# Sigmoid attention with a gated FFN on one core: where batch 0's first FFN chunks stand among its scores and value products

## The chip, the core and the metric

One core of one Trainium2 chip runs the whole program. The metric is the device time in microseconds from one execution; runs are given by their median. TensorE (PE) does the matrix products, ScalarE (ACT) the sigmoids, VectorE (DVE) most copies out of PSUM, GpSimd (POOL) issues the loads, SyncE (SP) the stores and DMA transposes. TensorE's weight loads are a row of their own (PEld) and overlap its matmuls.

## The reference

```python
def _attn_ref(q, k, v):                       # batch 8, heads 12, seq 448, head_dim 64
    scores = scale * np.matmul(q, k.transpose(0, 1, 3, 2)) - np.log(S)
    attn = 1.0 / (1.0 + np.exp(-scores))
    return np.matmul(attn, v)

def _moe_ref(x, w_gate, w_val, w_out):        # x: 3584 x 768, d_ff 1536
    gate = np.maximum(x @ w_gate, 0.0)
    val = x @ w_val
    return gate * val @ w_out
```

The attention output, with its heads joined, is x. Each score goes through a sigmoid by itself, so there is no sum over a row and no rescaling: a value product can begin as soon as the sigmoids of its first keys are done. Inputs and result are 32-bit floats; the kernel computes in 16-bit floats with 32-bit sums.

## The kernel before

**Attention.** A batch has 12 heads, taken as three groups g of four heads; a head's 448 positions are 7 chunks of 64. The scores are made with the keys on the partitions: four matmuls of 64x64 weights at a time, one in each quarter of the array (`qk`, L232). Queries and keys must first be turned (`pe_transposes`, L194): matmuls against an identity into PSUM, then copied to `qkT` by VectorE. ScalarE's sigmoid (L186) takes the scores from PSUM to a 16-bit tile `PT`. The value product (`pv`, L248) runs over the 7 key chunks in order, 28 matmuls in two banks; VectorE scales the two banks into `xT` (`put_xT`, L176), the FFN's input.

**FFN.** d_ff is 12 chunks f of 128. For a chunk, `gv` makes the gate product and the value product (six matmuls each over the 768 input features, one bank each), then the relu of the gate and the product of the two, which goes to `hT`. Batches 0 and 1 make their chunks this way. From batch 2 on other functions (`gv_pair`, `down_pair`) do it for two batches together; they are not touched here.

**Batch 0 in slots.** Nothing is there to overlap with at the start, so batch 0 is cut finer: its queries into a first part of 256 columns and a second of 192. There are six slots (`FirstSlot`, L269): slots 0, 1, 2 are groups 0, 1, 2 with the first query part, slots 3, 4, 5 the same groups with the second. A slot has four units of two key chunks (the last has one): a unit makes scores into one of two pairs of PSUM banks (`pairp`, two buffers), and one sigmoid takes them out. A slot's value product needs the sigmoids of all its four units. Chunk f of the FFN for the first query part needs the value products of slots 0, 1 and 2; chunk f for the second part needs those of slots 3, 4 and 5.

**What sets the order.** The program is scheduled by hand: each engine does its instructions in the order in which the code emits them, and waits at an instruction whose inputs or buffers aren't ready. The order around the change is the table `after`: its entry (i, u) is what is emitted behind unit u of slot i. `ffn_mix(n)` takes n chunks from the queue `gv_queue`. Matrix products other than the units' scores take PSUM banks from a ring of four (`bank`), each reused four takes later. For the first four chunks relu and product are both done by VectorE (`act_relu` False).

**Loads.** All loads of batch 0, of the gate and value weights (`load_gv`, in pieces by chunks: 0 and 1, 2 and 3, 4 and 5, 6 to 8, 9 to 11) and of batch 1 are issued by GpSimd ahead of this stretch in its own order. From the ninth on, a load is issued when the eighth before it has landed.

Of the kernel before, what the change touches and what calls it, by code (L numbers as in the profile page):

```python
# [17 lines left out]
def kernel(  # L18
# [10 lines left out]
    nc = tc.nc  # L29
# [5 lines left out]
    P = 128  # L35
    NCH = S // 64
    NDC = DM // P
# [3 lines left out]
    HALVES = ((0, QCUT), (QCUT, NCH))  # L41
# [34 lines left out]
    def bank(name, shape=(P, 512), dtype=FP32):  # L76
        pool, tag = free[0]
        free.rotate(-1)
        return pool.tile(list(shape), dtype, tag=tag, name=name)
# [60 lines left out]
    wg = wpool.tile([P, NDC, DF], FP16, name="wg")  # L140
    wv = wpool.tile([P, NDC, DF], FP16, name="wv")
# [26 lines left out]
    xT_tiles = {}  # L168
# [25 lines left out]
    def pe_transposes(b, g, ti, c0=0, c1=NCH):  # L194
        transposed(b, g, ti, c0, c1)()

    def transposed(b, g, ti, c0, c1):
        t16 = in_tiles[b][ti]
        qkT = qkT_of(b, g)
        trt = bank16("trt")  # L200
        for c in range(c0, c1):
            for h in range(2):
                nc.tensor.transpose(  # L203
                    trt[64 * h : 64 * h + 64, c * P : (c + 1) * P],
                    t16[:, 2 * g + h, c * D : (c + 1) * D],
                    ident[:],
                )

        def copy(a0=c0, a1=c1):
            nc.vector.tensor_copy(  # L210
                qkT[:, ti * NCH + a0 : ti * NCH + a1, :].rearrange("p c x -> p (c x)"),
                trt[:, a0 * P : a1 * P],
            )

        return copy
# [92 lines left out]


    def gv(b, q0, qn, f, act_relu):  # L310
        gv_out(b, q0, qn, f, act_relu, [gv_product(b, q0, qn, f, i) for i in range(2)])

    def gv_two(b, q0, qn, f):
        ps = [[gv_product(b, q0, qn, f + u, i) for u in range(2)] for i in range(2)]
        for u in range(2):
            gv_out(b, q0, qn, f + u, False, (ps[0][u], ps[1][u]))

    def gv_product(b, q0, qn, f, i):
        ps = bank(("g_ps", "v_ps")[i])
        for dc in range(NDC):  # L320
            nc.tensor.matmul(  # L321
                ps[:, 0:qn],
                (wg, wv)[i][:, dc, f * P : (f + 1) * P],
                xT_tiles[b][:, dc, q0 : q0 + qn],
                start=(dc == 0),
                stop=(dc == NDC - 1),
            )
        return ps

    def gv_out(b, q0, qn, f, act_relu, ps):  # L330
        gate_sb = gsbp.tile([P, S], FP32, tag="gsb", name="gate_sb")
        if act_relu:
            nc.scalar.activation(gate_sb[:, 0:qn], ps[0][:, 0:qn], AF.Relu)
        else:
            nc.vector.tensor_scalar(
                out=gate_sb[:, 0:qn], in0=ps[0][:, 0:qn], scalar1=0.0, scalar2=None, op0=AOP.max
            )
        g = b // 2
        if g not in hT_tiles:
            hT_tiles[g] = hTp.tile([P, NFC, 2 * S], FP16, tag="hT", name="hT")  # L340
        o = (b % 2) * S + q0
        nc.vector.tensor_tensor(  # L342
            out=hT_tiles[g][:, f, o : o + qn],
            in0=gate_sb[:, 0:qn],
            in1=ps[1][:, 0:qn],
            op=AOP.mult,
        )
# [316 lines left out]
    gv_queue = deque()  # L664

    def push_gv(b, q0, qn, fs, act_relu=True):
        for f in fs:
            gv_queue.append(lambda f=f: gv(b, q0, qn, f, act_relu))

    def push_first(half, fs, act_relu=True):  # L670
        c0, c1 = HALVES[half]
        push_gv(0, 64 * c0, 64 * (c1 - c0), fs, act_relu)

    def ffn_mix(count, hooks=()):
        hooks = list(hooks)
        for left in range(count, -1, -1):
            while hooks and hooks[0][0] >= left:
                hooks.pop(0)[1]()
            if left:
                gv_queue.popleft()()  # L680
# [14 lines left out]
    other_keys()  # L695
    keep_warm(2, S // 2)
    slots = [FirstSlot(half * NG + g, g, half) for half in range(2) for g in range(NG)]
    push_first(0, range(0, 2), False)
    gv_queue.append(lambda: gv_two(0, 0, 64 * HALVES[0][1], 2))
    def second_queries():  # L700
        for g in range(1, NG):
            pe_transposes(0, g, 1, QCUT, NCH)
# [5 lines left out]
    def first_of_second_batch():  # L708
        pe_transposes(1, 0, 1)
        keys = transposed(1, 0, 0, 0, NCH)  # L710
        keys(0, 3)
        keys(3, NCH)

    def pv_then_queries():
        slots[2].pv()
        second_queries()

    def two_pv():
        slots[3].pv()
        slots[4].pv()  # L720


    after = {
# [9 lines left out]
        (2, 1): lambda: pe_transposes(0, 0, 1, QCUT, NCH),  # L733
        (2, 2): slots[0].pv,
        (2, 3): slots[1].pv,
        (3, 0): pv_then_queries,
        (3, 2): lambda: ffn_mix(1),
        (4, 0): lambda: ffn_mix(1),
        (4, 2): lambda: ffn_mix(1),
        (5, 0): two_pv,  # L740
        (5, 2): first_of_second_batch,
    }
    for i, slot in enumerate(slots):
        for u in range(4):
# [202 lines left out]
```

## Time and profile before

| | |
|---|---|
| median of 3 runs | 391.79 us (391.43 to 391.85) |
| the profiled execution | 392.69 us, its span 390.9 us |
| mean granted TensorE clock | 0.998 |
| busiest groups of TensorE | scores 48.0 us (756 matmuls), value products 37.2 us (756), chunks of `gv` 66.5 us (432) |
| DMA moved | 43.79 MB, mean 112 GB/s |
| loads, issue to landing | 6.1 to 13.1 us for keys, 5.9 to 12.3 us for queries within the first 60 us |

A line of the profile names the engine, the code line, the operation, what it writes and reads by the program's names (`xT<-pv_ps`), its shape and its count. In the view by time a line begins with start and length in us, and what stands in brackets is the idle time before it and what ended that. Lines of equal operation are merged, and a merged line can hold waits that show only in the chain of waits, which follows the work that ended last, from step to step. The end of a matmul is modelled, so two matmul lines overlap by some 0.2 us; from start to start is the safer measure.

### The profile page before, as it was taken

To read this page: it belongs to the slowest core of one execution; us is meant where nothing else is said; L and a number is where in the kernel's file an instruction comes from. 1 tells how busy PE (TensorE), PEld (TensorE's weight loads), DVE (VectorE), ACT (ScalarE), POOL (GpSimd) and SP (SyncE) were. 2 spreads that over 40 slices of the span, in tenths; PEclk is the share of its full clock that TensorE was granted. 3 is DMA by queue.
4 is the path that set the end of the run, shared out by engine and by line. 5 is a ranking of instruction groups with operands and counts; after the bars stand their busy time and mean duration, and the time that the engine had idled before them with its cause. 6 is when DMAs were issued, how large, how long until landed. Compare 5 with 4: busy or idle time off the path is not lost.

```text
span 390.9 us, 8798 instructions
## 1 busy us (share of the span) xinstructions
PE 384.7 (98%) x3504; PEld 218.0 (56%) x3504; DVE 283.4 (73%) x560; ACT 228.4 (58%) x483; POOL 50.1 (13%) x74
## 2 busy tenths in 40 slices
PE   8999999999999999999999999999999999999995
PEld 6678776445455545454555554545455555555663
DVE  3453444358387789999757789999987788999563
ACT  5967786784877755555556774545467354333321
POOL 8643404300320300003000300000000000000000
PEclk9999999999999999999999999999999999999999
DMA  9999997996998992225946696132003220000335
GB/s 174 198 199 204 204 186 120 205 204 111 194 185 166 140 236 37 49 47 58 195 93 115 136 198 108 24 67 41 14 18 74 74 80 2 0 3 0 81 88 155
DMA packets 68985, 43.79 MB, mean 112 GB/s; under 512 B 35664, under 2 KB 65616, under 8 KB 68944
## 3 DMA queue, kind: packets, MB, share of 16 engines
q0 software_dynamic: 30496, 23.24, 39.6%
q1 hardware_dynamic: 37664, 19.24, 24.1%
q10 hardware_dynamic: 784, 0.75, 0.6%
q8 instruction: 27, 0.44, 0.5%
q14 instruction: 14, 0.11, 0.1%
HBM read 47.19 MB, written 11.01 MB: 149 GB/s over the span
## 4 chain that ended last, share of the span: by engine, by line
PE 93%; DMA 4%; DVE 1%; POOL 1%; issue 0%; ACT 0%; POOLq 0%; DVEq 0%; ACTq 0%
PE u L408 33%; PE g L408 16%; PE y L408 10%; PE qk_ps L238 9%; PE pv_ps L256 7%; PE g_ps L321 7%; PE v_ps L321 7%; DMA wv<-in_moe_w_val_dram 3%; DMA k<-in_k_dram 2%; PE ya L369 1%; PE trt L203 1%; PE yb L369 1%; ACT PT L186 0%; DVE ysb L478 0%; POOL wg L148 0%
## 5 line engine op out<-in xcount | busy, mean ns | idle before, releaser
L186 ACT ACTIVATE PT<-qk_ps 128x448 f16<-128x448 f32 (+3 forms) x318 | 151.0, 585 | 75.2 <-PE qk_ps L238 75.0
L408 PEld LDWEIGHTS <-S 128*128 128x128 f16 x558 | 54.6, 98 | 44.7
L620 DVE TENSOR_TENSOR gsb<-g,gsb 128x448 f32<-128x448 f32 x72 | 42.9, 625 | 10.3 <-PE g L408 9.7
L238 PE MATMUL qk_ps<-qkT 64*64 64x448 f16 (+2 forms) x756 | 48.0, 337 | 0.5 <-ACT PT L186 0.3
L342 DVE TENSOR_TENSOR hT<-gate_sb,v_ps 128x256 f16<-128x256 f32 (+2 forms) x36 | 16.4, 465 | 35.5 <-PE v_ps L321 17.9
L408 PEld LDWEIGHTS <-hT 128*128 128x128 f16 x306 | 28.7, 98 | 22.3 <-issue 4.9
L616 ACT COPY gsb<-u 128x448 f32<-128x448 f32 x48 | 25.6, 557 | 24.0 <-PE u L408 22.9
L460 ACT ACTIVATE ysb<-u 128x384 f32<-128x384 f32 x31 | 15.2, 491 | 38.2 <-PE u L408 33.8
L256 PE MATMUL pv_ps<-PT,v 64*64 64x448 f16 (+2 forms) x756 | 37.2, 329 | 0.0
L183 DVE TENSOR_SCALAR xT<-pv_ps 128x448 f16<-128x448 f32 (+2 forms) x53 | 27.8, 567 | 10.9 <-PE pv_ps L256 9.8
L321 PE MATMUL v_ps<-xT,wv 128*128 128x256 f16 (+2 forms) x216 | 33.2, 290 | 0.5 <-DMA wv<-in_moe_w_val_dram 0.5
L321 PE MATMUL g_ps<-xT,wg 128*128 128x256 f16 (+2 forms) x216 | 33.3, 291 | 0.0
L408 PEld LDWEIGHTS <-wg 128*128 128x128 f16 x216 | 20.1, 98 | 21.8 <-issue 4.3
L408 PEld LDWEIGHTS <-wv 128*128 128x128 f16 x216 | 21.1, 98 | 19.7
L238 PEld LDWEIGHTS <-qkT 64*64 64x64 f16 x756 | 18.2, 106 | 21.2 <-issue 14.9
L478 DVE SCALAR_TENSOR_TENSOR ysb<-y,ysb 128x384 f32<-128x384 f32 x29 | 16.1, 556 | 17.9 <-PE y L408 10.4
L256 PEld LDWEIGHTS <-v 64*64 64x64 f16 x756 | 22.3, 107 | 10.6 <-issue 0.8
L408 PE MATMUL u<-T,hT 128*128 128x384 f16 x132 | 25.1, 326 | 0.0
L110 POOL DMA_DIRECT2D k<-in_k_dram x14 | 10.8, 773 | 111.0 <-DVE rel L221 104.2
L321 PEld LDWEIGHTS <-wg 128*128 128x128 f16 x216 | 18.8, 98 | 10.8 <-issue 4.5
L321 PEld LDWEIGHTS <-wv 128*128 128x128 f16 x216 | 20.1, 98 | 8.2 <-DMA wv<-in_moe_w_val_dram 0.8
L408 PE MATMUL u<-xT,wg 128*128 128x448 f16 x108 | 23.5, 354 | 0.0
(78 smaller groups left out, 536.4 us busy)
## 6 DMA issues: line engine op xcount, KB each, us to landing
out_dram<-ysb SPq DMA_DIRECT2D x52, 192.0 KB, 2.9
v<-in_v_dram POOLq DMA_DIRECT2D x8, 336.0 KB, 14.5
v<-in_v_dram POOLq DMA_DIRECT2D x16, 168.0 KB, 14.4
k<-in_k_dram POOLq DMA_DIRECT2D x4, 672.0 KB, 12.0
q<-in_q_dram POOLq DMA_DIRECT2D x4, 672.0 KB, 15.6
k<-in_k_dram POOLq DMA_DIRECT2D x9, 224.0 KB, 11.9
q<-in_q_dram POOLq DMA_DIRECT2D x7, 224.0 KB, 12.2
wo<-in_moe_w_out_dram POOLq DMA_DIRECT2D x1, 1536.0 KB, 12.0
```

The source lines that it names most:

```text
L110: nc.gpsimd.dma_start(t16[:, xs, cs], rows_of(src, b)[:, xs, cs])
L183: nc.vector.tensor_scalar(out=xT, in0=src, scalar1=XSCALE, scalar2=None, op0=AOP.mult)
L186: nc.scalar.activation(PT_ap, ps_ap, AF.Sigmoid, bias=sig_bias, scale=qk_scale)
L238: nc.tensor.matmul(out_of(hh)[o : o + 64, :], qkT[rows, c, cols], qkT[rows, NCH + c0 : NCH + c1, cols], start=True, stop=True, tile_positi ...
L256: nc.tensor.matmul(ps[hh][64 * r : 64 * r + 64, 0:qn], v16[rows, 2 * g + hh, c * D : (c + 1) * D], pieces[c][rows, hh, :], start=(c == 0), ...
L321: nc.tensor.matmul(ps[:, 0:qn], (wg, wv)[i][:, dc, f * P : (f + 1) * P], xT_tiles[b][:, dc, q0 : q0 + qn], start=(dc == 0), stop=(dc == ND ...
L342: nc.vector.tensor_tensor(out=hT_tiles[g][:, f, o : o + qn], in0=gate_sb[:, 0:qn], in1=ps[1][:, 0:qn], op=AOP.mult,)
L408: nc.tensor.matmul(ps[:, 0:n], A[:, k_, :], W[:, k_, :], start=(first and k_ == 0), stop=(k_ == kn - 1), skip_group_check=True,)
L460: nc.scalar.activation(o, ps[:, 0:HM], AF.Copy, scale=OUT_SCALE)
L478: nc.vector.scalar_tensor_tensor(out=o, in0=ps[:, 0:HM], scalar=OUT_SCALE, in1=o, op0=AOP.mult, op1=AOP.add)
L616: by(gs[u][i][:], ps[u][:, 0:S])
L620: nc.vector.tensor_tensor(out=gs[u][i][:], in0=ps[u][:, 0:S], in1=gs[u][i][:], op=AOP.add)
```

## The change

The order of batch 0's second half is another one, and the chunks 2 and 3 are no longer made as a pair with their gate products first.

| behind | before | after |
|---|---|---|
| slot 3 unit 0 | value product of slot 2, query transposes | |
| slot 3 unit 1 | | value product of slot 2 |
| slot 3 unit 2 | chunk 0 | query transposes |
| slot 3 unit 3 | | value product of slot 3 |
| slot 4 unit 0 | chunk 1 | |
| slot 4 unit 1 | | chunk 0 |
| slot 4 unit 2 | chunks 2 and 3, paired | |
| slot 4 unit 3 | | chunk 1, value product of slot 4 |
| slot 5 unit 0 | value products of slots 3 and 4 | |
| slot 5 unit 1 | | chunk 2 |
| slot 5 unit 2 | batch 1's transposes | |
| slot 5 unit 3 | | batch 1's transposes, chunk 3 |
| then | value product of slot 5 | value product of slot 5 |

"Query transposes" are the 12 of groups 1 and 2 for the second query part, "batch 1's transposes" the 28 of its group 0, queries ahead of keys.

```diff
--- before.py
+++ after.py
@@ -308,26 +308,17 @@
 
 
     def gv(b, q0, qn, f, act_relu):
-        gv_out(b, q0, qn, f, act_relu, [gv_product(b, q0, qn, f, i) for i in range(2)])
-
-    def gv_two(b, q0, qn, f):
-        ps = [[gv_product(b, q0, qn, f + u, i) for u in range(2)] for i in range(2)]
-        for u in range(2):
-            gv_out(b, q0, qn, f + u, False, (ps[0][u], ps[1][u]))
-
-    def gv_product(b, q0, qn, f, i):
-        ps = bank(("g_ps", "v_ps")[i])
-        for dc in range(NDC):
-            nc.tensor.matmul(
-                ps[:, 0:qn],
-                (wg, wv)[i][:, dc, f * P : (f + 1) * P],
-                xT_tiles[b][:, dc, q0 : q0 + qn],
-                start=(dc == 0),
-                stop=(dc == NDC - 1),
-            )
-        return ps
-
-    def gv_out(b, q0, qn, f, act_relu, ps):
+        ps = []
+        for nm, wt in (("g_ps", wg), ("v_ps", wv)):
+            ps.append(bank(nm))
+            for dc in range(NDC):
+                nc.tensor.matmul(
+                    ps[-1][:, 0:qn],
+                    wt[:, dc, f * P : (f + 1) * P],
+                    xT_tiles[b][:, dc, q0 : q0 + qn],
+                    start=(dc == 0),
+                    stop=(dc == NDC - 1),
+                )
         gate_sb = gsbp.tile([P, S], FP32, tag="gsb", name="gate_sb")
         if act_relu:
             nc.scalar.activation(gate_sb[:, 0:qn], ps[0][:, 0:qn], AF.Relu)
@@ -695,8 +686,7 @@
     other_keys()
     keep_warm(2, S // 2)
     slots = [FirstSlot(half * NG + g, g, half) for half in range(2) for g in range(NG)]
-    push_first(0, range(0, 2), False)
-    gv_queue.append(lambda: gv_two(0, 0, 64 * HALVES[0][1], 2))
+    push_first(0, range(0, 4), False)
     def second_queries():
         for g in range(1, NG):
             pe_transposes(0, g, 1, QCUT, NCH)
@@ -711,13 +701,13 @@
         keys(0, 3)
         keys(3, NCH)
 
-    def pv_then_queries():
-        slots[2].pv()
-        second_queries()
-
-    def two_pv():
-        slots[3].pv()
-        slots[4].pv()
+    def ffn_then_pv(i):
+        ffn_mix(1)
+        slots[i].pv()
+
+    def transposes_then_ffn():
+        first_of_second_batch()
+        ffn_mix(1)
 
 
     after = {
@@ -733,12 +723,13 @@
         (2, 1): lambda: pe_transposes(0, 0, 1, QCUT, NCH),
         (2, 2): slots[0].pv,
         (2, 3): slots[1].pv,
-        (3, 0): pv_then_queries,
-        (3, 2): lambda: ffn_mix(1),
-        (4, 0): lambda: ffn_mix(1),
-        (4, 2): lambda: ffn_mix(1),
-        (5, 0): two_pv,
-        (5, 2): first_of_second_batch,
+        (3, 1): slots[2].pv,
+        (3, 2): second_queries,
+        (3, 3): slots[3].pv,
+        (4, 1): lambda: ffn_mix(1),
+        (4, 3): lambda: ffn_then_pv(4),
+        (5, 1): lambda: ffn_mix(1),
+        (5, 3): transposes_then_ffn,
     }
     for i, slot in enumerate(slots):
         for u in range(4):
```

## The prediction

> **What bounds the kernel now.** I read the page's busy times and chain first, then the list of waits of TensorE, then TensorE and ScalarE in order of time between 14 and 32 us (the only stretch whose program the change touches), then the DMA issues of that stretch.
>
> ```profile
> PE 384.7 (98%) x3504; PEld 218.0 (56%) x3504; DVE 283.4 (73%) x560; ACT 228.4 (58%) x483; POOL 50.1 (13%) x74
> PE 93%; DMA 4%; DVE 1%; POOL 1%; issue 0%; ACT 0%; POOLq 0%; DVEq 0%; ACTq 0%
> ```
>
> TensorE is busy for 98% of the span and makes 93% of the chain. So the order of the other engines' work costs only what it makes TensorE wait, and a wait removed early comes out at the end, if none replaces it. TensorE's waits in the whole span are three:
>
> ```profile
> PE warm_ps L174 <- DVE zeros L129: 1.2, 1, 1.2
> PE v_ps L321 <- DMA wv<-in_moe_w_val_dram: 0.5, 1, 0.5
> PE qk_ps L238 <- ACT PT L186: 0.3, 1, 0.3
> ```
>
> The first and third lie before the changed stretch. The second is chunk 0's value product. TensorE in order of time (start, length):
>
> ```profile
> 18.26 0.52 PE L238 MATMUL qk_ps<-qkT 64*64 64x192 f16 x16
> 18.71 0.83 PE L321 MATMUL g_ps<-xT,wg 128*128 128x256 f16 x6
> 20.09 0.83 PE L321 MATMUL v_ps<-xT,wv 128*128 128x256 f16 x6 [0.54 <-DMA wv<-in_moe_w_val_dram]
> 20.84 0.44 PE L238 MATMUL qk_ps<-qkT 64*64 64x192 f16 x12
> 21.22 0.83 PE L321 MATMUL g_ps<-xT,wg 128*128 128x256 f16 x6
> 21.88 0.82 PE L321 MATMUL v_ps<-xT,wv 128*128 128x256 f16 x6
> 22.63 0.52 PE L238 MATMUL qk_ps<-qkT 64*64 64x192 f16 x16
> ```
>
> Chunk 1 shows the undisturbed pace: its value product starts 0.66 us after its gate product (21.22 to 21.88), and the next thing 0.75 later (21.88 to 22.63), so a chunk is 1.41 us. Chunk 0's value product should have started at 18.71 + 0.66 = 19.37 and started at 20.09: a wait of **0.72 us** (the 0.54 counts from the modelled end of the matmul before). Sixteen score matmuls of this form take 0.46 (22.63 to 23.09 in the same view), so a unit of eight takes 0.23.
>
> The list of waits hides a second loss, inside a group. It shows in the chain of waits at the last value product:
>
> ```profile
> 28.91 0.33 PE pv_ps L256 x16
> 29.24 0.01 issue
> 29.25 0.36 PE pv_ps L256 x8
> 29.61 0.02 issue
> 29.63 0.28 PE pv_ps L256 x4
> 29.91 0.57 PE qk_ps L238 x12
> ```
>
> The sixteen first take 0.33, so eight should take 0.17 and four 0.08: 28 matmuls are 0.58, which the pair of value products before it confirms (56 from 26.08 to 27.24, 1.16). Eight took from 29.25 to 29.63 instead of 0.17 (0.21 lost), and they began 0.17 late after sixteen that started, in the timeline, at 28.74. That is **0.38 us** of waiting, and the cause stands on ScalarE:
>
> ```profile
> 17.22 0.81 ACT L186 ACTIVATE PT<-qk_ps 128x768 f16<-128x768 f32 x1 [0.18 <-PE qk_ps L238]
> 18.73 1.51 ACT L186 ACTIVATE PT<-qk_ps 128x768 f16<-128x768 f32 x2 [0.70 <-PE qk_ps L238]
> 27.69 1.90 ACT L186 ACTIVATE PT<-qk_ps 128x768 f16<-128x768 f32 x3 [0.29 <-PE qk_ps L238]
> ```
>
> The last three sigmoids of slot 5 run back to back until 27.69 + 1.90 = 29.59, and the last four matmuls go 0.04 later. Two chained sigmoids of 768 last 1.51, one 0.81, so one follows the other by 0.70; one of 384 is 1.90 - 2 x 0.70 = 0.50 long.
>
> **What the change removes.** Chunk 0 moves behind the fourth slot's value product. By the schedule below its value product starts at 21.1; its weights landed at 20.04 (issued 9.56, 10.48 us in the chain of waits), so the 0.72 goes. Chunk 3 (1.41 us) now stands between slot 5's last sigmoid and the last value product: the 0.38 goes, as the cover is over three times the wait. Together -1.10.
>
> **What it adds.** I lay the new order out with those prices from 16.68, where slot 3's first unit starts in the same view and up to which nothing changes.
> Slot 3's unit 0 ends at 16.91 and unit 1 follows at once. It needs the score banks of slot 2's unit 3 (two pairs of banks in turn), whose sigmoid ended at 17.03 (twelve from 6.96 for 10.07): it starts at 17.08, **0.17 waited**. Behind it in TensorE's queue stands everything. Slot 2's value product, 0.82 (slot 0's, 14.98 to 15.80), ends at 18.13; unit 2, 18.36; twelve query transposes, 0.46 (17.80 to 18.26), 18.82; unit 3, 18.94. ScalarE gets these units sooner than it can work: sigmoids from 17.22 every 0.70 give unit 2 an end of 19.43 and unit 3 one of 17.22 + 3 x 0.70 + 0.50 = 19.82. Slot 3's value product starts at 18.94, does four key chunks to 19.27, waits for unit 2 until 19.48 (0.21), does two to 19.65, waits for unit 3 until 19.87 (0.22), and ends at 19.95: **0.43 waited**.
> Then, with no wait that I can find: two units 20.41, chunk 0 21.82, two units (twelve matmuls, 0.38 as from 20.84 to 21.22) 22.20, chunk 1 23.61, slot 4's value product 24.19, two units 24.65, chunk 2 26.06, two units 26.44, batch 1's 28 transposes (0.90 in the chain) 27.34, chunk 3 28.75, last value product 29.33. Before, batch 1's scores begin at 29.71 in the timeline; so **-0.38 us**. By terms: -1.10 + 0.17 + 0.43 + 0.09 = -0.41, where 0.09 is one more step from a full-array chunk to quarter-array matmuls (0.75 against 0.66; four such steps where there were three). I take -0.4.
>
> The other edits I cost at nothing. Splitting the pair: twelve gate and twelve value matmuls take 1.32 and 1.40 from 23.09 to 25.81, which is two chunks of 1.41 less 0.1, the step already counted. Its cover was the value weights of chunks 2 and 3, issued at 11.18 and landing 12.9 later, at 24.08; chunk 2's value product now starts at 25.3. Without that cover each us late costs a us. VectorE gets the same instructions in another order (0.42 a piece) and is at 73%; chunk 3's two end before the last value product's copies are due, and the four rotating banks are each free 0.3 us or more before reuse, except slot 3's value product, whose two banks VectorE empties from 18.15 to 18.91, just in time. ScalarE gets nothing new. No DMA is issued in the moved steps; GpSimd's loads of the stretch wait for earlier landings alone, and SyncE issues nothing between 0.74 and 52.58 us.
>
> Bounds. The 0.60 added on ScalarE: at least the 0.38 that its only like row shows, at most one sigmoid step more, 1.30; I take the chain's, as every start in it is a measured step. The extra step: 0 to 0.4 (four steps at 0.09, if every boundary of the finer mix costs). The removed 0.72 is one execution's; the three runs of before differ by 0.42, so I let it be 0.3 to 1.1.
>
> **Baseline.** The profiled execution took 392.69 us, of which the span is 390.9; -0.4 makes these 392.3 and 390.5. The runs' median is 391.79, 0.9 below the profiled time, and takes the same shift: 391.4.
>
> **Rivals.** *The queries come late (the other side).* Batch 1's transposes move from 27.73 to 26.44, and their query half lands just then:
>
> ```profile
> wv<-in_moe_w_val_dram POOLq DMA_DIRECT2D x1, 384.0 KB, 12.9
> q<-in_q_dram POOLq DMA_DIRECT2D x1, 224.0 KB, 11.6
> ```
>
> Issued at 14.72, it lands at 26.3, 0.1 ahead. Before had 1.4 to spare. If it lands over 0.5 us later than here, the change is a loss: with the 13.1 that the slowest key load takes, it lands at 27.8, TensorE waits 1.4, and the time is 392.8. For it: a margin of 0.1 while the DMA share by stretch stands at 1.3 to 1.45 from 6 us on. Against: landings in this stretch follow each other evenly.
> *The weight wait is not there without the profiler.* Unprofiled runs are 0.9 faster; if the 0.72 is part of that, only 0.38 is removed against 0.69 added: 392.1. Against: 0.72 is no rounding, and transfers fill the engines from 2 us on (share 0.96 and more in every stretch of 2 us).
> *ScalarE's debt is smaller than I chain it.* If slot 3's value product does not wait, 391.79 - 1.10 + 0.17 + 0.09 = 390.95. Against it is the last value product of before, which did wait.
> *The clock falls.* The 22 warm-up matmuls at the start (194 columns) took 3.74 us, 0.17 each; those of 192 columns later take 0.49 for six, 0.08. [...] From 16.9 to 20.3 the new order has 0.6 of waits and 0.46 of transposes with no full-array matmul. Against: from 17.8 to 21.2 before has 0.72 and 0.46, and the granted clock there is 1.00.
> [...]
>
> **How the numbers follow.** Forecast 391.4: 0.54, itself from 390.9 to 392.0. Late queries 0.14, hidden weight wait 0.18, small debt 0.10, clock 0.04. A measurement of this kernel can tell 0.2%, 0.78 us, from no change: below 391.0 or above 392.6. Below: 0.12 of the forecast and 0.08 of the small debt, 0.20. Above: late queries 0.08, clock 0.04, and 0.05 of the rest, 0.17. The range 390.8 to 392.5 leaves out about 0.2.
>
> **What would show it.** No wait for wv in the new trace, and chunk 0 beginning near 20.4. Slot 3's value product stretched from 0.58 to about 1.0 with sigmoids back to back from 17.2 to 19.8. The last value product 0.58 long. Batch 1's scores beginning near 29.3, and TensorE's order the same from there. I am wrong if batch 1's transposes wait for q, if the granted clock dips near 20 us, or if a later wait takes the 0.4 back.

## The result, and the profile after

| | median | runs | |
|---|---|---|---|
| before | 391.73 us | 6 (391.43 to 391.85) | |
| after | 393.20 us | 6 (393.04 to 393.41) | ratio 1.0039, 95% interval 1.0026 to 1.0052 |

The change makes the kernel slower by 1.5 us; 391.4 was forecast, with 392.5 as the upper end. The profiled execution of the changed kernel took 393.05 us, its span 391.3. The page still shows TensorE as the bound:

```profile
PE 384.3 (98%) x3504; PEld 217.7 (56%) x3504; DVE 283.5 (72%) x560; ACT 228.2 (58%) x483; POOL 50.1 (13%) x74
PE 93%; ACT 3%; DVE 1%; DMA 1%; issue 1%; DVEq 0%; ACTq 0%
```

The wait for value weights is gone from the chain, as forecast (DMA 4% became 1%), and "issue" has come in with 1%. The list of TensorE's waits names it:

```profile
PE warm_ps L174 <- DVE zeros L129: 1.2, 1, 1.2
PE qk_ps L238 <- issue: 1.1, 1, 1.1
PE qk_ps L238 <- ACT PT L186: 0.3, 1, 0.3
```

One new wait of 1.1 us, in scores, that nothing in the profile released. In order of time, TensorE after the change:

```profile
15.39 0.96 PE L256 MATMUL pv_ps<-PT,v 64*64 64x256 f16 x28
16.16 0.83 PE L238 MATMUL qk_ps<-qkT 64*64 64x192 f16 x16
16.79 0.96 PE L256 MATMUL pv_ps<-PT,v 64*64 64x256 f16 x28
...
18.30 0.28 PE L238 MATMUL qk_ps<-qkT 64*64 64x192 f16 x4
18.41 1.15 PE L256 MATMUL pv_ps<-PT,v 64*64 64x192 f16 x28
19.36 0.36 PE L238 MATMUL qk_ps<-qkT 64*64 64x192 f16 x7
20.85 0.43 PE L238 MATMUL qk_ps<-qkT 64*64 64x192 f16 x9 [1.13 <-issue]
21.22 0.83 PE L315 MATMUL g_ps<-xT,wg 128*128 128x256 f16 x6
21.89 0.82 PE L315 MATMUL v_ps<-xT,wv 128*128 128x256 f16 x6
...
29.56 0.77 PE L256 MATMUL pv_ps<-PT,v 64*64 64x192 f16 x28
30.16 0.74 PE L238 MATMUL qk_ps<-qkT 64*64 64x448 f16 x12
```

Slot 4's first two units, sixteen matmuls, stop after the seventh and go on at 20.85. They last from 19.36 to 21.22, 1.86 us, where sixteen take 0.46: **1.40 us** lost, in the middle of a unit, on a matmul that waits for no semaphore. The last value product takes 0.60 (29.56 to 30.16) and no longer waits. From batch 1's first scores on, everything is as before: the span ends 361.1 us after them, before 361.2, and in all the runs below 361.1 to 361.2. So the time is read from the moment at which batch 1's scores begin.

### The profile page after: what moved, and what is told of

It is laid out like the page before. It is cut to its first block, busy times and chain, and to the rows that moved or that the text cites. A ratio compares the mean times of both kernels' runs of the same rounds, so it can differ in the third digit from the quotient of the medians.

```text
span 391.3 us, 8798 instructions
## 1 busy us (share of the span) xinstructions
PE 384.3 (98%) x3504; PEld 217.7 (56%) x3504; DVE 283.5 (72%) x560; ACT 228.2 (58%) x483; POOL 50.1 (13%) x74
## 4 chain that ended last, share of the span: by engine, by line
PE 93%; ACT 3%; DVE 1%; DMA 1%; issue 1%; DVEq 0%; ACTq 0%
PE u L399 33%; PE g L399 16%; PE y L399 10%; PE qk_ps L238 9%; PE pv_ps L256 8%; PE g_ps L315 8%; PE v_ps L315 7%; ACT PT L186 3%; PE ya L360 1%; DMA ysb<-in_k_dram 1%; PE trt L203 1%; PE yb L360 1%; DVE ysb L469 0%; DVE qkT L210 0%; DVE S L390 0%
## 5 line engine op out<-in xcount | busy, mean ns | idle before, releaser
L238 PEld LDWEIGHTS <-qkT 64*64 64x64 f16 x756 | 18.4, 106 | 22.4 <-issue 16.1
```

Source lines behind the costliest of these rows:

```text
L238: nc.tensor.matmul(out_of(hh)[o : o + 64, :], qkT[rows, c, cols], qkT[rows, NCH + c0 : NCH + c1, cols], start=True, stop=True, tile_positi ...
```

## The experiments

Two readings were open. *Instruction fetch:* the page of before has a DMA queue of the kind "instruction" (packets, MB, share of the 16 engines' span):

```profile
q8 instruction: 27, 0.44, 0.5%
```

The packets are 16,384 bytes each; TensorE executes 7015 instructions (matmuls, weight loads and seven of its sequencer), about 260 to a packet. By this reading TensorE's program comes in blocks, and TensorE had run out of one until 20.85 us. *A hidden dependency:* slot 4's scores wait for something that the trace doesn't name. The runs below are all compared with before; where an edit is made to the changed kernel, the text says so.

**The kernel before, a second time** (no edit).

> The kernel before, once more. Both theories: the wait of chunk 0's value product for its weights is smaller than the 0.72 us of the first profile, 0.1 to 0.3 us, and the span is near 390.0 us, because its three first runs were 0.9 us below their profiled one. If the wait is again 0.7 and the span 390.9, the profiled execution was typical, and the rival 'the weight wait is not there without the profiler' falls.

One execution, 391.79 us, span 390.0. TensorE at the start of the stretch, around chunk 0 and at the end of the stretch:

```profile
15.72 0.96 PE L256 MATMUL pv_ps<-PT,v 64*64 64x256 f16 x28
...
18.45 0.83 PE L321 MATMUL g_ps<-xT,wg 128*128 128x256 f16 x6
19.12 0.82 PE L321 MATMUL v_ps<-xT,wv 128*128 128x256 f16 x6
19.87 0.53 PE L238 MATMUL qk_ps<-qkT 64*64 64x192 f16 x12
...
27.85 1.17 PE L256 MATMUL pv_ps<-PT,v 64*64 64x192 f16 x28
28.82 0.76 PE L238 MATMUL qk_ps<-qkT 64*64 64x448 f16 x12
```

Gate to value 0.67, value to scores 0.75: chunk 0 doesn't wait at all, not even the 0.1 us that was the least expected. Its weights had landed at 18.86, against 20.04 in the first profile. The 0.72 us belonged to one execution, whose batch 1 began at 29.71 instead of 28.82 and which took 392.69 instead of 391.7. Since this run was profiled as well, profiling alone does not make the wait. In the five further traces below that have chunk 0 at its old place, its value product starts 0.66 to 0.74 after its gate product, so it waits for 0.08 at most. The last value product waits as in the first profile (27.85 to 28.82 is 0.97, 0.58 of it work).

**Fewer instructions ahead of the stretch.** In the changed kernel the warm-up matmuls at the start (`keep_warm`, products of zeros) are made fewer and longer: 17 matmuls with their 17 weight loads go.

```diff
-    keep_warm(22, 194)
+    keep_warm(10, 427)
-    keep_warm(2, S // 2)
+    keep_warm(1)
-        (0, 1): lambda: keep_warm(4, S // 2),
+        (0, 1): lambda: keep_warm(2),
-        (1, 0): lambda: keep_warm(4, S // 2),
+        (1, 0): lambda: keep_warm(2),
```

> The changed kernel with its warm-up matmuls fewer and longer (same columns, 34 TensorE instructions fewer ahead of the stretch). Theory, instruction fetch: TensorE's instructions come in blocks of 256, and in the changed kernel it reaches the next block before the block is there. Then the wait stays at the same number in TensorE's stream (705 to 706) and so lies 34 instructions later in the work, inside chunk 0 instead of among slot 4's scores; it shrinks from 1.1-1.4 us to 0.4-0.8, and the time falls by 0.5 to 0.9 us, to some 392.5. Rival, something that slot 4's scores wait for (a sigmoid, a bank, a copy) and that the trace does not name: the wait stays at slot 4's scores with its 1.1 us, and the time stays at 393.2.

392.89 us, ratio to before 1.0028 (1.0018 to 1.0038). The scores of slot 4 no longer stop; chunk 0 does:

```profile
20.34 0.83 PE L315 MATMUL g_ps<-xT,wg 128*128 128x256 f16 x6
21.00 0.38 PE L315 MATMUL v_ps<-xT,wv 128*128 128x256 f16 x2
22.24 0.61 PE L315 MATMUL v_ps<-xT,wv 128*128 128x256 f16 x4 [0.86 <-issue]
```

With TensorE's instructions counted in the trace, matmuls and weight loads alike, the first after the stop is number 706 here and number 706 in the changed kernel, though it is the weight load of a score there and of chunk 0's value product here. The wait goes with the number in the stream, not with the work: the hidden dependency falls. The size was missed, in the time (392.5 expected) and in the stop: 1.0 us remained (21.11 to 22.24 from start to start is 1.13, 0.11 of it the matmul before), not 0.4 to 0.8, because the packet, too, came later (19.73 against 18.41, in the table below).

**Chunk 0 ahead of slot 3's value product,** in the changed kernel.

```diff
-        (3, 3): slots[3].pv,
-        (4, 1): lambda: ffn_mix(1),
+        (3, 3): lambda: ffn_then_pv(3),
```

> The changed kernel with chunk 0 ahead of slot 3's value product, right behind unit 3, instead of behind slot 4's unit 1. Theory, instruction fetch: 24 instructions that take 1.4 us stand before the block's end in place of scores, so TensorE gets there later: the wait falls from 1.1-1.4 to 0.3-0.7 us, at the same instruction number, now inside slot 3's value product; and that product no longer waits for its sigmoids (0.4). Time 391.9 to 392.3. Rival, a wait that belongs to slot 4's scores: it stays there, and only the 0.4 goes: 392.8.

A miss in the total (391.9 to 392.3 expected): 393.67 us, ratio 1.0046 (1.0031 to 1.0061).

```profile
20.18 0.69 PE L256 MATMUL pv_ps<-PT,v 64*64 64x192 f16 x23
21.12 0.35 PE L256 MATMUL pv_ps<-PT,v 64*64 64x192 f16 x5 [0.25 <-issue]
21.23 0.57 PE L238 MATMUL qk_ps<-qkT 64*64 64x192 f16 x16
22.60 0.36 PE L238 MATMUL qk_ps<-qkT 64*64 64x192 f16 x8 [0.80 <-ACT PT L186]
23.30 0.28 PE L238 MATMUL qk_ps<-qkT 64*64 64x192 f16 x4 [0.34 <-ACT PT L186]
```

The stop did shrink, to about 0.5 us from start to start (20.63 to 21.12), and stands at number 706 again, now inside slot 3's value product. But with chunk 0 gone from between slot 4's units 1 and 2, unit 2 waits for its banks until the sigmoid of unit 0 is done (0.80), and unit 3 for that of unit 1 (0.34).

**Loads held back until about 15 us** in the changed kernel (the issue of the weights and of batch 1's loads moved behind a copy that waits for slot 2's query transposes).

```diff
-    load_gv(0, 2)
-    load_gv(2, 4)
...
+    def other_loads():
+        nc.gpsimd.tensor_copy(gate[0:1, :], qkT_tiles[(0, 0)][0:1, NCH + QCUT, 0:2])
+        load_gv(0, 2)
...
-        (2, 1): lambda: pe_transposes(0, 0, 1, QCUT, NCH),
+        (2, 1): lambda: (pe_transposes(0, 0, 1, QCUT, NCH), other_loads()),
```

> The changed kernel with the weights' and batch 1's loads held back until slot 2's query transposes are copied (about 15 us), so that few transfers are under way when TensorE's next block is asked for. Theory, instruction fetch slowed by the loads: the fetch packet starts within about 1 us of 15.5 instead of at 18.4, and the wait among slot 4's scores is gone or under 0.3 us; the loads come 1 to 2 us later, so waits for wv and q of up to 1 us may appear further on. Rival, a wait of slot 4's scores for other work: it stays at 1.1 us. Rival, the fetch is slow whatever the loads do: the packet still starts 3 us after the block before was entered, and the wait stays.

One execution, 395.01 us. The DMA queues of the changed kernel by stretch: first from 15.4 to 18.3 us, then from 18.4 to 19.4 (packets, MB, share; the share adds up the packets' times, which overlap, so it can pass 100%):

```profile
q0 software_dynamic: 1137, 0.57, 145.5%
```

```profile
q0 software_dynamic: 374, 0.18, 137.4%
q8 instruction: 1, 0.02, 5.9%
```

TensorE enters the block before, whose first instruction is number 450 (706 less 256, the distance between the stops at 706 and 962 in the table below), at 15.42, and for three us only loads move; the instruction packet starts at 18.41. With the loads held back, from 15.4 to 16.6 us:

```profile
q8 instruction: 1, 0.02, 4.8%
```

The packet starts at 15.60, with no load beside it, and TensorE does not stop at number 706:

```profile
18.43 1.15 PE L259 MATMUL pv_ps<-PT,v 64*64 64x192 f16 x28
19.38 0.52 PE L241 MATMUL qk_ps<-qkT 64*64 64x192 f16 x16
20.15 0.83 PE L318 MATMUL g_ps<-xT,wg 128*128 128x256 f16 x6 [0.24 <-DMA wg<-in_moe_w_gate_dram]
22.10 0.83 PE L318 MATMUL v_ps<-xT,wv 128*128 128x256 f16 x6 [1.13 <-DMA wv<-in_moe_w_val_dram]
```

The sixteen scores go through in one piece, and the chunk behind them starts late only by its wait for the gate weights. The time is lost to loads that now come late: TensorE waits for the weights of chunk 0 (0.24 and 1.13), the value weights of chunk 2 (0.37) and batch 1's queries (1.05). The same trace holds the opposite case: the next block, that of number 706, is entered at 19.49, when the loads run again (1335 packets, 0.67 MB, from 19.5 to 23.0), and the next instruction packet starts at 23.11, 3.6 us later. So it is the loads that delay the start of the packet: 0.2 us after the entry without them, 3.6 with them, and 3.0 in the changed kernel (15.42 to 18.41). The first two come from one execution.

**The change's last part alone, and undone.** In the table of the change the last part is chunk 3 behind batch 1's transposes and ahead of the last value product. First the kernel before with chunk 3 at the end and chunk 2 moved ahead of slot 3's value product:

```diff
-    push_first(0, range(0, 2), False)
-    gv_queue.append(lambda: gv_two(0, 0, 64 * HALVES[0][1], 2))
+    push_first(0, range(0, 4), False)
...
     def two_pv():
+        ffn_mix(1)
         slots[3].pv()
...
-        (4, 2): lambda: ffn_mix(1),
+        (5, 3): lambda: ffn_mix(1),
```

> The kernel before with the change's last part alone: chunk 3 between batch 1's transposes and the last value product (chunk 2 then stands by itself ahead of slot 3's value product). By the prediction's terms only the last value product's wait goes, 0.4 us: 391.3. Instruction fetch says otherwise: the next block (TensorE's instruction 962) was there at about 27.05 us in the second run of before, just when TensorE asked for it (27.03); with chunk 3's 1.4 us taken from ahead of it, TensorE asks at about 25.7 and waits 1.2 to 1.4 us inside batch 1's transposes, so the time is 392.4 to 392.9, slower than before.

393.09 us, ratio 1.0031 (1.0020 to 1.0042): slower, but not where expected. TensorE reached number 962 at 27.5 and did not stop there. With no chunk between slot 4's units 2 and 3 it waited for ScalarE instead, from 21.63 on:

```profile
22.96 0.28 PE L238 MATMUL qk_ps<-qkT 64*64 64x192 f16 x4 [0.81 <-ACT PT L186]
23.67 0.36 PE L238 MATMUL qk_ps<-qkT 64*64 64x192 f16 x8 [0.42 <-ACT PT L186]
```

So it was made again with chunk 2 left where it keeps ScalarE its time:

```diff
-    push_first(0, range(0, 2), False)
-    gv_queue.append(lambda: gv_two(0, 0, 64 * HALVES[0][1], 2))
+    push_first(0, range(0, 4), False)
...
+        (5, 3): lambda: ffn_mix(1),
```

> The kernel before with chunk 3 alone moved between unit 3 of slot 5 and the last value product; chunk 2 stays between slot 4's units 2 and 3, so that ScalarE keeps its time, and the transposes stay behind unit 2. By the prediction's terms the last value product's wait goes: 391.3 to 391.4. Instruction fetch: 1.4 us of work with few instructions are gone from ahead of TensorE's instruction 962, which it now reaches at about 25.6 us, while the block is there at about 27.0; a wait of 1.1 to 1.4 us stands in batch 1's transposes at that number, and the time is 392.4 to 392.8.

392.65 us, ratio 1.0020 (1.0011 to 1.0029).

```profile
23.02 0.83 PE L321 MATMUL v_ps<-xT,wv 128*128 128x256 f16 x6 [0.19 <-DMA wv<-in_moe_w_val_dram]
...
26.11 0.33 PE L203 MATMUL trt<-ident,k 128*64 128x128 f16 x5
27.05 0.47 PE L203 MATMUL trt<-ident,k 128*64 128x128 f16 x9 [0.60 <-issue]
```

The stop stands in the transposes, and the first instruction after it is number 962 = 706 + 256. It is 0.8 us and not 1.1 to 1.4, since chunk 2's value weights, no longer covered by a second gate product, cost 0.35 ahead of it (22.00 to 23.02 is 1.02, against 0.67).

Then the changed kernel with its last part undone:

```diff
-        (5, 1): lambda: ffn_mix(1),
-        (5, 3): transposes_then_ffn,
+        (5, 1): lambda: ffn_mix(2),
+        (5, 2): first_of_second_batch,
```

> The changed kernel with the last part undone: chunk 3 right behind chunk 2, batch 1's transposes behind unit 2, and the last value product directly behind unit 3. The fetch wait at instruction 706 stays at 1.3 to 1.4 us (theory: nothing ahead of it changes), and the last value product waits for its sigmoids again, 0.4 us: 393.5 to 393.7. If that wait does not come back, ScalarE was not its cause.

393.37 us, ratio 1.0035 (1.0022 to 1.0049).

```profile
20.80 0.43 PE L238 MATMUL qk_ps<-qkT 64*64 64x192 f16 x9 [1.08 <-issue]
...
30.24 0.28 PE L256 MATMUL pv_ps<-PT,v 64*64 64x192 f16 x4 [0.16 <-ACT PT L186]
```

The stop at 706 stays, and the last value product waits for its sigmoids again (29.42 to 30.32, 0.90 instead of 0.60). The total moved by 0.17 from the changed kernel's 393.20, less than that 0.3 and within the interval, so the return is read from the trace and not from the time.

**Chunk 0 put back,** in the changed kernel.

```diff
-        (3, 2): second_queries,
+        (3, 2): lambda: (second_queries(), ffn_mix(1)),
-        (4, 3): lambda: ffn_then_pv(4),
+        (4, 3): slots[4].pv,
```

> The changed kernel with chunk 0 put back behind slot 3's unit 2 (with the query transposes ahead of it), the other chunks one place earlier each. If only the wait at instruction 706 mattered, it falls from 1.4 to about 0.5 us, slot 3's value product no longer waits for its sigmoids, and the time is 391.8 to 392.1. Instruction fetch with blocks that come some 6.2 us apart while loads fill the queues, whenever they are asked for: TensorE then meets the block after it too early as well, at instruction 962, which is there at about 27.0; a second wait of 0.6 to 0.9 us appears there, and the time is 392.4 to 392.8.

392.87 us, ratio 1.0026 (1.0015 to 1.0036): in the second range, by another way.

```profile
21.49 0.35 PE L256 MATMUL pv_ps<-PT,v 64*64 64x192 f16 x5 [0.36 <-issue]
...
24.85 0.66 PE L256 MATMUL pv_ps<-PT,v 64*64 64x192 f16 x12 [0.56 <-ACT PT L186]
```

The stop at 706 fell to 0.6 (20.89 to 21.49 from start to start), but slot 4's value product, with no chunk ahead of it, waited for its sigmoids; number 962 was reached at 27.97, and no second stop stands there.

**Three tries for a faster kernel,** all from the kernel before: the transposes behind slot 5's unit 3; then chunks 2 and 3 apart and slots 3's and 4's value products behind unit 1; then that with the gate products of both chunks at the first place and the value products of both at the second. They are called x8, x10 and x11 here; the second diff is that of x10 and x11, in which the queue holds single chunks or the two halves of the pair.

```diff
-        (5, 2): first_of_second_batch,
+        (5, 3): first_of_second_batch,
```

```diff
-        (5, 0): two_pv,
-        (5, 2): first_of_second_batch,
+        (5, 0): lambda: ffn_mix(1),
+        (5, 1): two_pv,
+        (5, 3): first_of_second_batch,
```

> The kernel before with batch 1's transposes behind slot 5's unit 3 instead of unit 2, and nothing else moved. They cover the last value product's wait for its sigmoids (0.9 us of work over 0.4), and no work is taken from ahead of instruction 962, so no fetch wait comes: 391.3 to 391.45, faster than before. If the wait for the sigmoids is not what the last value product loses, or if VectorE's copies of the transposes now hold batch 1's first scores, it stays at 391.7 or gets slower.

> The kernel before with chunks 2 and 3 apart (behind slot 4's unit 2 and slot 5's unit 0), slots 3's and 4's value products behind slot 5's unit 1, and batch 1's transposes behind its unit 3. Meant to meet three limits at once: no unit waits for its banks, the last value product finds its sigmoids done (0.3 to 0.4 us less), and TensorE reaches instruction 962 at about 27.3, after its block. 391.4 to 391.6; at or above 391.9 if one of the three is still missed.

> x10_spread with the gate products of chunks 2 and 3 together behind slot 4's unit 2 and their value products together behind slot 5's unit 0, so that the value weights have landed when they are needed. The 0.44 us that x10_spread waited for them goes, nothing else changes: batch 1's scores begin 0.3 us earlier than in the second run of before, TensorE reaches instruction 962 at about 27.1, just after its block, and the time is 391.4 to 391.7. If the block is late again, a wait of 0.1 to 0.4 stands at instruction 962 and the time is that of before.

x8: 392.42 us, 1.0011 (1.0002 to 1.0020). x10: 392.00, 1.0004 (0.9995 to 1.0013). x11: 392.00, 1.0005 (0.9996 to 1.0014). In x8 the transposes had been covering unit 3's wait for its banks, which now shows; in x10 the value weights are late; x11 has neither:

```profile
27.67 0.28 PE L238 MATMUL qk_ps<-qkT 64*64 64x192 f16 x4 [0.74 <-ACT PT L186]
```

```profile
23.21 0.83 PE L321 MATMUL v_ps<-xT,wv 128*128 128x256 f16 x6 [0.28 <-DMA wv<-in_moe_w_val_dram]
```

```profile
23.61 0.52 PE L238 MATMUL qk_ps<-qkT 64*64 64x192 f16 x12
24.07 1.48 PE L326 MATMUL v_ps<-xT,wv 128*128 128x256 f16 x12
...
28.16 0.77 PE L256 MATMUL pv_ps<-PT,v 64*64 64x192 f16 x28
28.83 0.76 PE L238 MATMUL qk_ps<-qkT 64*64 64x448 f16 x12
```

In x11 the list of waits names none of TensorE's in the stretch, and batch 1's scores begin at 28.83, as in before (28.82). The 0.4 us of waiting came back in small pieces, mostly where one kind of matmul follows another: twelve scores ahead of a chunk take 0.46 here, ahead of a value product 0.27 (24.92 to 25.19 in the second run of before), the last value product 0.67 behind transposes, 0.58 without its wait in before, and one more chunk half ends in scores (0.09): 0.37 together. What makes up each piece no run here takes apart. None of the three was faster than before: x8 was slower, x10 and x11 can't be told from it.

The stops together, times from the traces (us). "Packet starts" is the start of the instruction packet on q8, "runs at" the first instruction after the stop:

```
kernel                    enters 450   packet starts   runs at   packet to run
changed                   15.42        18.41           20.85     2.44   at 706
fewer instructions        16.38        19.73           22.24     2.51   at 706
chunk 0 first             15.68        18.64           21.12     2.48   at 706
last part undone          15.42        18.43           20.80     2.37   at 706
chunk 0 put back          16.07        18.95           21.49     2.54   at 706
chunk 3 last              (706: 21.55) 24.57           27.05     2.48   at 962
loads held back           15.44        15.60           no stop (706 at 19.49)
before, second run        15.75        18.45           no stop (706 at 21.75)
```

## Why the prediction was wrong

**The step that failed** is "Then, with no wait that I can find: two units 20.41". Those two units hold the 1.40 us. The schedule priced every semaphore, bank and landing, and took TensorE's own instructions for granted. Before, TensorE spent 6.0 us on the 256 instructions from 450 to 706 (15.75 to 21.75 in its second run), because chunks 0 and 1 stand among them, each 1.41 us for 24 instructions. The change takes both chunks out of that block and puts in slot 3's value product and more scores. A chunk's instructions take 59 ns each on average (1.41 us for 24), those of the changed block 16 (4.06 us for 256, waits included); TensorE is through by 19.48, 4.1 us after entering, and the next block takes 5.4 (15.42 to 20.85) while loads fill the queues. The second run of before meets number 962 at 27.03, with its packet started at 24.60; by the 2.4 to 2.5 us of the table that is just when the block is there, and the kernel with chunk 3 alone moved to the end, which reaches it sooner, stops at it. The chunks among the scores do two things at once in this kernel: they are the work, and they are the time in which instructions arrive.

The stops stand at 706 and 962, 256 instructions apart, and last 0.5 to 1.4 us in six runs. No stop stands at 706 with the loads held back, nor in before, where the loads run but TensorE spends 6.0 us on the block.

**The term that was mis-sized** is the 0.72 removed: 0 in the second run of before, 0.08 at most in five more traces. The text let it be 0.3 to 1.1, too narrow, and set -0.4 from the one slow execution against a median that does not contain it. The rival "the weight wait is not there without the profiler" gave 392.1, and 391.73 with the 0.26 that remain of the terms below without the stop makes 392.0: its size was right, its reason was not.

**What held.** From the start of slot 1's value product to batch 1's scores, before took 13.10 us (15.72 to 28.82) and after 14.77 (15.39 to 30.16): +1.67. The terms: the stop +1.40; slot 3's unit 1 +0.17 (its sixteen scores from 16.16 to 16.79, 0.63 for 0.46; 0.17 forecast); slot 3's value product +0.37 (18.41 to 19.36, 0.95 for 0.58; 0.43 forecast); the last value product -0.37 (0.38 forecast); one more step +0.09. Sum +1.66; smaller pieces, of up to 0.13 us, cancel. Without the stop an estimated 0.26 of loss remain, so the change would not have been faster even then: what the change removes at the end it pays for on ScalarE in slot 3. This execution entered the stretch 0.33 earlier than that run of before, for which the change is no reason (nothing ahead of it moved); the medians differ by 1.47.

**The other rivals.** Batch 1's queries landed at 25.27, and their transposes began at 27.24: no wait. No run shows the fall of the clock, to which the forecast gives 0.04. The chunk behind the stop takes 1.41 us (21.22 to 22.63), as chunk 1 did in before, and the granted clock stayed at 1.00 around the stop, where TensorE was busy for 2.26 us of 3.40 (it reads 1.00 in before from 0 to 3.3 us too, over warm-up matmuls of 0.17 us each, so the lengths say more):

```profile
17.50:20.90 3.40, 2.26 (x74) 1.47 (x67) 1.91 (x6) 1.73 (x3) 1.21 (x2) 1.00 1.46 198
```

The pair of chunks 2 and 3, costed at nothing, did cover something once the order moved: chunk 2 alone at its old place waited 0.35 to 0.44 for its value weights. In the change itself it stands late enough, and its cost there was nothing, as forecast.

## What to carry to other kernels

Before small matmuls are moved next to each other, count TensorE's instructions, weight loads too, between block boundaries and the time spent on them: here the next 256 instructions needed 5.4 us while loads filled the queues, and one long chunk among them is worth more than its place in the dependency graph says (chunk 0 among them took the stop from 1.40 to 0.5 us). Where a short unit between two engines has only two buffers, work taken from between its steps can turn into a wait there, as it did in three runs (0.80 and 0.34 us with chunk 0 ahead of slot 3's value product, 0.81 and 0.42 with chunk 2 moved away from slot 4's units, 0.74 in x8). And a wait that one profile shows (0.72 us here, none in the second) has to be found in a second profile before a change is built, or costed, on its removal.

## What the hardware showed that was not expected

While loads fill the queues, TensorE's instruction packets start some 6.2 us apart (18.41, 24.57 and 30.73 in the changed kernel; 18.45, 24.60 and 30.62 in the second run of before; 5.8 to 6.5 between 18 and 32 us in every trace with the loads at their old place), though TensorE enters its blocks at other times in each; with the loads held back one started 0.2 us after the block before was entered. Between the start of a packet and the first instruction of its block lie 2.4 to 2.5 us in all six stops, of which the packet itself moves for 0.9 to 1.0. It moved for 0.93 with no load beside it, so the loads delay its start and not its transfer. What fills the rest, why the packets keep that rhythm, and why the boundaries lie at 450, 706 and 962 and not at multiples of 256, no run here shows.
